# The last step's down products: the third PSUM bank from a pair of the up products

## The chip, the cores and the metric

The kernel runs on one core of a Trainium2 chip. The time is the device time of the whole program in microseconds (us); the medians are over several executions, and the profile is of one execution. PSUM is the memory that the matmuls write to; the kernel uses it as eight banks. The engines are TensorE (PE in the views; PEld is its load of a matmul's first operand, the weight load), VectorE (DVE), ScalarE (ACT), GpSimd (POOL) and SyncE (SP).

## The reference, cut to what matters

```python
# per batch and head: a linear attention with an RMS norm; x is its output, 4608 x 512
kv  = np.einsum('bhsd,bhse->bhde', k, v)
out = np.einsum('bhsd,bhde->bhse', q, kv)
x   = out / rms * g_norm                      # reshaped to (4608, 512)
# four experts, summed with the tokens' probabilities
for e in range(E):
    h = np.maximum(x @ w1[e], 0.0)            # "up",   512 -> 1024
    out += p[:, e:e + 1] * (h @ w2[e])        # "down", 1024 -> 512
```

All is float32. The change touches only the down product of the very last step.

## The kernel before

The work is 36 steps: 4 experts by 9 chunks of 512 tokens. (The prediction calls the last one step 35, its index from 0.) Each matrix product is made of seven smaller ones, numbered 1 to 7, from sums and differences of blocks. So the relu'd blocks h1, h2, ... need further adds: h3 = h2 - h6, for instance. Some of the products are split by seven once more (the "inner" products). A *merge* scales a finished product by the tokens' probabilities and adds it into the output rows, which frees its bank. A *pass* is one matmul record of the profile: each float32 matmul of the kernel shows as two.

A small list-scheduler in the kernel lays all operations out in order of time. A buffer belongs to a kind, and each kind has some slots. An operation can be placed only when a slot of the kind it needs is free, and an add marked `either` goes to VectorE or GpSimd, whichever the plan reaches first. So moving one buffer to another kind can reorder operations that the change does not name.

```python
BANKS = {"u1": 2, "u2": 2, "db": 2, "ab": 2}      # eight PSUM banks in four pairs
...
bank = {1: Buf("u1", ...), 2: Buf("u2", ...), 5: Buf("u2", ...)}        # up()
...
def either(n):
    return {"DVE": 0.155 + 0.00104 * n, "POOL": 0.15 + 0.00225 * n}
...
elif m == 4:                                                            # up(), the last part
    add(key, unit(2), made[1], made[4])             # h2; adds default to `either`
    relu(key, h[2])
    add(key, unit(3), h[2], h[6], ALU.subtract)     # h3
...
def down(s, e, c):            # each expert's last chunk, and all chunks of expert 0
    for t in range(2):        # two halves of the tokens
        for j, m in enumerate((1, 6, 5, 7, 4, 3, 2)):
            kind = "ab" if e and t else "db"
            if m == 1:
                banks[1] = Buf(kind, f"d1_{s}_{t}")      # holds products 1, 6, 7, 4
            elif m in (2, 5):
                banks[2] = Buf(kind, f"d{m}_{s}_{t}")    # 5 and then 3; for 2 a new one
            ps = banks[1 if m in (1, 6, 7, 4) else 2]
            ...  # four matmuls into ps[:, 0:256]; then a merge on VectorE into the output rows
```

The step just ahead of the last one uses the inner products. Its final group also lives in `db`: there the inner products 7 and then 4 share one bank, and between them ScalarE must copy 7 out (a "snapshot"). Other inner products hold the other bank.

Of the kernel before, what the change touches and what calls it, by code (L numbers as in the profile page):

```python
# [230 lines left out]
def kernel(  # L231
# [39 lines left out]
    E, DM, F = moe_w1.shape  # L271
# [5 lines left out]
    NCH = B + 1  # L277
# [58 lines left out]
    def pe(products, columns, passes=2):  # L336
        return {"PE": passes * products * (0.008 + 0.0008125 * columns) + 0.003}
# [506 lines left out]
    def four(b):  # L844

        return b.ap[:].rearrange("p (a b u t) -> p a b u t", a=2, b=2, u=2)
# [230 lines left out]
    def down(s, e, c):  # L1077
        h = hidden.pop(s)
        base = s + 1.2
        merge, send = result(s, e, c, base)  # L1080
        second = []
        for t in range(2):
            banks = {}
            for j, m in enumerate(MERGED):
                key = base + (7 * t + j + 0.5) / 14
                kind = "ab" if e and t else "db"
                if m == 1:
                    banks[1] = Buf(kind, f"d1_{s}_{t}")
                elif m in (2, 5):
                    banks[2] = Buf(kind, f"d{m}_{s}_{t}")  # L1090
                ps = banks[1 if m in (1, 6, 7, 4) else 2]

                def product(eng, m=m, t=t, ps=ps):
                    for kt in range(4):
                        nc.tensor.matmul(  # L1095
                            ps.ap[:, 0:HN], lhsT=four(h[m])[:, kt // 2, t, kt % 2, :],
                            rhs=w2f[e][m].ap[:, kt * HN:(kt + 1) * HN],
                            start=(m in (1, 2, 5) and kt == 0), stop=(kt == 3),
                            skip_group_check=True,
                        )  # L1100

                op = plan.add(
                    key, pe(4, HN), product, reads=[h[m], w2f[e][m]], writes=[ps],
                    after=second[-1:] if t and m in (1, 5) else (),
                )
                op.marks = ps, HN
                if m == 2:
                    second.append(op)
                i, half, fresh = {
                    1: (t, 0, True), 2: (t, 0, False), 6: (t, 1, True), 3: (t, 1, False),  # L1110
                    5: (2 + t, 1, True), 7: (2 + t, 1, False), 4: (2 + t, 0, True),
                }[m]
                merge(key - 0.4, [ps], lambda ps=ps: ps.ap[:, 0:HN], i, half, fresh)
            send(base + 0.5 * (t + 1), t)
            send(base + 0.5 * (t + 1), 2 + t)
# [171 lines left out]
    for e in range(E):  # L1287
        for c in range(NCH):
            s = e * NCH + c
# [14 lines left out]
            if e and c < NCH - 1:  # L1304
                if not primed:
                    banks = [Buf("ab", f"prime{i}") for i in range(2)]

                    def prime(eng, banks=banks):
                        for b in banks:
                            nc.tensor.matmul(b.ap[:, 0:P], lhsT=ident[:], rhs=ident[:], start=True,  # L1310
                                             stop=False, skip_group_check=True)
                            nc.tensor.matmul(b.ap[:, P:HN], lhsT=ident[:], rhs=ident[:], start=False,
                                             stop=True, skip_group_check=True)

                    primed.append(plan.add(s + 1.1, pe(4, P), prime, writes=banks))
                    primed[0].marks = banks[0], HN
                down_deep(s, e, c)
            else:
                down(s, e, c)
# [54 lines left out]
```

## Time and profile before

| | |
|---|---|
| time, median of 3 runs | 1731.64 us (1731.56 to 1731.66) |
| profiled span | 1729.4 us |
| TensorE busy | 1719.6 us, 99% |
| TensorE's share of the chain that ended last | 99% |
| from product 7's block (1698.08) to the start of the last merge (1724.86) | 26.78 us |
| from there to the end of the span (the trace has it as 1729.43) | 4.6 us |

The stretch that the change can touch starts at four passes of the previous step's product 7, line L1170, and ends with the last merge (line L1049). I call it the *tail*; starts are printed to 0.01 us, so a tail can be off by 0.01. Timelines give the start of an instruction or a merged run of them, its length in us, the engine, the line, what it writes and reads, and in brackets how long the engine was idle before it and who ended that.

### The profile page before, as it was taken

To read this page: it belongs to the slowest core of one execution; us is meant where nothing else is said; L and a number is where in the kernel's file an instruction comes from. 1 tells how busy PE (TensorE), PEld (TensorE's weight loads), DVE (VectorE), ACT (ScalarE), POOL (GpSimd) and SP (SyncE) were. 2 spreads that over 40 slices of the span, in tenths; PEclk is the share of its full clock that TensorE was granted. 3 is DMA by queue.
4 is the path that set the end of the run, shared out by engine and by line. 5 is a ranking of instruction groups with operands and counts; after the bars stand their busy time and mean duration, and the time that the engine had idled before them with its cause. 6 is when DMAs were issued, how large, how long until landed. Compare 5 with 4: busy or idle time off the path is not lost.

```text
span 1729.4 us, 38448 instructions
## 1 busy us (share of the span) xinstructions
PE 1719.6 (99%) x15334; PEld 1652.0 (96%) x15334; DVE 1222.8 (71%) x1968; ACT 938.6 (54%) x2300; POOL 616.5 (36%) x561
## 2 busy tenths in 40 slices
PE   9999999999999999999999999999999999999998
PEld 7699999999999999999999999999999999999997
DVE  4755655565676777777788877777788877777774
ACT  3354544454444565656555556566555556665652
POOL 3421323133334333333345333333345333333331
PEclk9999999999999999999999999999999999999999
DMA  9756444633333343534465344444475344444442
GB/s 240 218 161 193 153 122 131 193 135 128 147 130 99 94 114 104 116 106 113 131 185 110 99 110 111 111 111 110 114 204 110 98 111 111 110 110 109 112 99 49
DMA packets 148596, 220.94 MB, mean 128 GB/s; under 512 B 49600, under 2 KB 90816, under 8 KB 148416
## 3 DMA queue, kind: packets, MB, share of 16 engines
q1 hardware_dynamic: 133312, 191.21, 35.6%
q0 software_dynamic: 15104, 27.27, 11.0%
q8 instruction: 120, 1.97, 0.5%
q14 instruction: 60, 0.49, 0.1%
HBM read 145.30 MB, written 73.14 MB: 126 GB/s over the span
## 4 chain that ended last, share of the span: by engine, by line
PE 99%; POOL 0%; ACT 0%; DVE 0%; issue 0%; POOLq 0%
PE u L881 45%; PE db L1170 19%; PE db L1095 15%; PE ab L1170 12%; PE ab L1095 2%; PE u L968 2%; PE ab L634 1%; PE ab L678 1%; PE ab L620 1%; PE ab L1323 1%; PE ab L660 1%; PE db L660 0%; POOL rt L551 0%; PE ab L722 0%; PE ab L704 0%; PE ab L738 0%
## 5 line engine op out<-in xcount | busy, mean ns | idle before, releaser
L360 DVE TENSOR_TENSOR big<-big,big 128x1024 f32<-128x1024 f32 (+1 forms) x449 | 440.9, 995 | 34.9 <-ACT big L864 23.8
L881 PE MATMUL u<-xf,big 128*128 128x128 f32 x3104 | 453.3, 276 | 0.0
L881 PEld LDWEIGHTS u<-xf,big 128*128 128x128 f32 x3104 | 401.5, 192 | 2.2
L881 PE MATMUL u<-xf,w1y 128*128 128x128 f32 x2652 | 389.9, 276 | 0.0
L908 DVE TENSOR_TENSOR big<-u,snap 128x256 f32<-128x256 f32 x430 | 181.3, 422 | 235.9 <-PE u L881 176.4
L881 PEld LDWEIGHTS u<-xf,w1y 128*128 128x128 f32 x2652 | 343.6, 192 | 2.1
L900 ACT ACTIVATE snap<-u 128x256 f32<-128x256 f32 x490 | 187.7, 383 | 251.6 <-PE u L881 212.2
L1095 PE MATMUL db<-big,big 128*128 128x256 f32 x1136 | 269.0, 382 | 2.1 <-DVE big L560 2.1
L1095 PEld LDWEIGHTS db<-big,big 128*128 128x128 f32 x1136 | 207.1, 192 | 25.4 <-DVE big L560 2.3
L900 ACT ACTIVATE big<-u 128x256 f32<-128x256 f32 x430 | 164.7, 383 | 110.6 <-PE u L881 75.5
L360 POOL TENSOR_TENSOR big<-big,big 128x256 f32<-128x256 f32 (+1 forms) x139 | 172.5, 1248 | 132.3 <-DVE big L360 46.8
L1170 PE MATMUL db<-big,big 128*128 128x128 f32 x1056 | 146.9, 276 | 0.4 <-ACT snap L1198 0.4
L864 ACT ACTIVATE big<-big 128x1024 f32<-128x1024 f32 x128 | 134.5, 1051 | 3.4 <-POOL big L360 2.1
L1170 PEld LDWEIGHTS db<-big,big 128*128 128x128 f32 x1056 | 132.1, 192 | 0.6 <-ACT snap L1198 0.6
L1236 POOL TENSOR_TENSOR big<-big 128x512 f32<-128x512 f32 x26 | 33.0, 1268 | 269.2 <-DVE big L360 263.9
L1198 ACT ACTIVATE snap<-db 128x256 f32<-128x256 f32 x192 | 68.4, 356 | 100.0 <-PE db L1170 95.1
L360 POOL TENSOR_TENSOR big<-big 128x512 f32<-128x512 f32 (+1 forms) x57 | 70.3, 1232 | 126.8 <-DVE big L360 102.6
L1170 PE MATMUL db<-kv,big 128*128 128x128 f32 x804 | 114.7, 275 | 0.0
L1065 POOL DMA_DIRECT2D out_dram<-big x100 | 91.2, 987 | 47.4 <-ACT snap L1198 22.8
L900 ACT ACTIVATE u<-u 128x256 f32<-128x256 f32 x245 | 90.9, 371 | 28.1 <-PE u L881 8.0
L1170 PEld LDWEIGHTS db<-kv,big 128*128 128x128 f32 x804 | 102.1, 192 | 0.1
L1206 DVE TENSOR_TENSOR big<-ab,snap 128x256 f32<-128x256 f32 x140 | 59.1, 422 | 57.4 <-ACT snap L1198 31.9
(213 smaller groups left out, 2676.9 us busy)
## 6 DMA issues: line engine op xcount, KB each, us to landing
xf<-x SPq DMA_DIRECT2D x108, 512.0 KB, 3.6
out_dram<-big POOLq DMA_DIRECT2D x84, 256.0 KB, 5.8
xf<-x_h SPq DMA_DIRECT2D x81, 256.0 KB, 3.2
xf<-x SPq DMA_DIRECT2D x81, 256.0 KB, 3.3
x<-xf SPq DMA_DIRECT2D x36, 512.0 KB, 6.1
big<-in_moe_w_dram SPq DMA_DIRECT2D x25, 512.0 KB, 4.8
small<-in_q_dram SPq DMA_DIRECT2D x72, 128.0 KB, 4.8
kv<-in_k_dram SPq DMA_DIRECT2D x30, 288.0 KB, 4.8
```

What stands on the lines that cost most here:

```text
L360: lambda eng: adder(eng).tensor_tensor(out=out_(), in0=a(), in1=b(), op=op),
L864: lambda eng: nc.scalar.activation(out=b.ap[:], in_=b.ap[:], func=ACT.Relu),
L881: nc.tensor.matmul(ps.ap[:, u * P:(u + 1) * P], lhsT=w1f[e][m][mm][1]()[:, u * P:(u + 1) * P], rhs=views[m][mm][1](), start=(mm in (1, 5) ...
L900: lambda eng: nc.scalar.activation(out=where(), in_=ps.ap[:, 0:HN], func=ACT.Copy),
L908: lambda eng: nc.vector.tensor_tensor(out=block(whole, a, t), in0=src.ap[:, 0:HN], in1=add_.ap[:], op=ALU.add),
L968: nc.tensor.matmul(bank.ap[:], lhsT=two(w.ap[:])[:, kt, ut * P:(ut + 1) * P], rhs=two(xh[dh].ap[:])[:, kt, :], start=(dh == kt == 0), stop ...
L1065: nc.gpsimd.dma_start(out=dst, in_=cell(i)[parts, :], accum_op=ALU.add)
L1095: nc.tensor.matmul(ps.ap[:, 0:HN], lhsT=four(h[m])[:, kt // 2, t, kt % 2, :], rhs=w2f[e][m].ap[:, kt * HN:(kt + 1) * HN], start=(m in (1, ...
L1170: nc.tensor.matmul(ps.ap[:, o * P:(o + 1) * P], lhsT=b.ap[:, col:col + P], rhs=w2q[e][m][mm][1]()[:, kt, :], start=(mm in (1, 5) and o == ...
L1198: lambda eng: nc.scalar.activation(out=where(), in_=group_of(ps.ap), func=ACT.Copy),
L1206: lambda eng: nc.vector.tensor_tensor(out=cell(tq, dq), in0=group_of(src.ap), in1=group_of(add_.ap), op=ALU.add,),
L1236: lambda eng: adder(eng).tensor_tensor(out=whole(to), in0=whole(a), in1=whole(b), op=ALU.add),
```

## The change

Its intent: the last step's products 5, 3 and 2 should not compete for the two `db` banks with the previous step's inner products. No up product follows, so the pair `u2` is idle.

```diff
                 elif m in (2, 5):
-                    banks[2] = Buf(kind, f"d{m}_{s}_{t}")
+                    banks[2] = Buf("u2" if s == E * NCH - 1 else kind, f"d{m}_{s}_{t}")
```

## The prediction

> **What bounds the kernel now.** I read the page's busy times and chain first, to see which engine sets the end; then the chain cut to the last 30 us, because the change touches only step 35 of 36; then the timeline of each engine there, for the size of every hole.
>
> ```profile
> PE 1719.6 (99%) x15334; PEld 1652.0 (96%) x15334; DVE 1222.8 (71%) x1968; ACT 938.6 (54%) x2300; POOL 616.5 (36%) x561
> PE 99%; POOL 0%; ACT 0%; DVE 0%; issue 0%; POOLq 0%
> ```
>
> TensorE works for 1719.6 of 1729.4 us and carries 99% of the chain. A change that removes no matmul can win at most the holes in its stream, 9.8 us over the whole span, and start and end of the program hold most of those. The chain at the end (start, duration, what):
>
> ```profile
> 1698.24 0.46 PE db L1170 x4
> 1698.70 0.02 issue
> 1698.72 0.28 ACT snap L1198
> 1699.01 0.04 issue
> 1699.05 1.16 PE db L1170 x8
> 1700.21 12.53 PE db L1095 x56
> 1712.74 12.10 PE ab L1095 x56
> 1724.84 0.02 issue
> 1724.86 0.48 DVE big L1049
> ```
>
> L1170 is the previous step's inner product, L1095 the last step's 14 down products of eight matmul passes. Equal numbers of passes took 12.53 and 12.10 us: a hole hides in the first seven. The TensorE timeline (start, us, what, idle before) and the weight loads size the holes:
>
> ```profile
> 1697.18 0.61 PE L1170 MATMUL db<-kv,big 128*128 128x128 f32 x4
> ...
> 1698.08 0.61 PE L1170 MATMUL db<-kv,big 128*128 128x128 f32 x4
> 1699.05 0.71 PE L1170 MATMUL db<-big,big 128*128 128x128 f32 x4 [0.36 <-ACT snap L1198]
> 1699.60 0.61 PE L1170 MATMUL db<-kv,small 128*128 128x128 f32 x4
> 1700.13 9.15 PE L1095 MATMUL db<-big,big 128*128 128x256 f32 x40
> ...
> 1712.57 8.80 PE L1095 MATMUL ab<-big,big 128*128 128x256 f32 x40
> ...
> 1705.56 3.32 PEld L1095 LDWEIGHTS db<-big,big 128*128 128x128 f32 x16 [0.39 <-DVE big L360]
> ```
>
> The undisturbed step from one block of four narrow passes to the next is 0.45 us (1697.18 to 1698.08 holds two such steps). So:
> - **Hole A**: the block at 1699.05 was due at 1698.53, 0.52 late. It then costs 0.55 to the next block instead of 0.45 (its first weight load is no longer hidden), 0.10 more. Together 0.62.
> - **Hole B**: the first down product was due at 1699.60 + 0.45 = 1700.05 and came at 1700.13, 0.08 late, plus about the same 0.10 for its exposed weight load: 0.18.
> - **Hole C**: 40 wide passes took 9.15 instead of 8.80, 0.35 more. 0.10 of it is B's weight load, so C is 0.25, at the weight load of 1705.56 that waited for a VectorE add.
>
> A + B + C = 1.05 us is all that exists in this stretch. The cause of C is one line of work:
>
> ```profile
> 1700.60 2.36 POOL L360 TENSOR_TENSOR big<-big,big 128x1024 f32<-128x1024 f32 x1 [0.69 <-ACT big L1042]
> 1702.99 1.06 ACT L864 ACTIVATE big<-big 128x1024 f32<-128x1024 f32 x1 [1.32 <-POOL big L360]
> 1704.29 1.22 DVE L360 TENSOR_TENSOR big<-big,big 128x1024 f32<-128x1024 f32 x1
> ```
>
> GpSimd forms h2, ScalarE applies the relu, VectorE forms h3 = h2 - h6, and product 3 waits for h3 until 1705.51 + 0.05.
>
> **What the skill says.** (1) PSUM — Partial Sum Buffer, section Terms: two engines must not be on one bank and quadrant at once, so a reused bank has to wait for its reader. The trace agrees in the ordering: A is product 4 of the previous step waiting until the snapshot of the same bank (0.28 us) is out, and B is the first down product waiting for that bank's next evacuation. (2) TensorE: Matmul & The Clock Gate, section The mechanism: matmuls are strictly in order, only weight loads are pulled ahead. The trace agrees: during A nothing else of TensorE's stream runs although product 5 of the last step had all its operands. What fills a hole must therefore stand in the hole in program order. (3) SBUF — State Buffer, section "SBUF: two separate sides": GpSimd and a VectorE operation with two SBUF inputs exclude each other on a shared port pair. A VectorE add of 128x512 (L1236) took 1.21 us beside a GpSimd add (1699.24, while GpSimd ran 1698.64 to 1699.91) and another of the same form 0.68 us alone (1702.97), so I ask below who is beside whom.
>
> **The change, part by part.** The list-scheduler lays the program out anew. Comparing both builds, all instructions up to the last step are the same and in the same order; the last 14 down products and a handful of neighbours move. No product, transfer or byte is added or removed.
>
> 1. *Product 5, first half, moves into hole A.* It now writes a bank of the second up pair, which no one uses, so it needs no wait and is placed between the previous step's products 7 and 4. Its 8 passes at 0.2157 (8.80 less the 0.38 tail of the last pass, over 39) last 1.73 us. Product 7 ends its issue at about 1698.52; product 4 then comes at about 1700.25, when the snapshot (out at 1699.00) is long done. A vanishes: -0.62.
> 2. *Hole B stays.* Products 4, 3 of the previous step and 1 of the last still use the same bank: issue of 4 ends 1700.69, 3 ends 1701.14, the copy of 4 starts about 0.31 after its last pass, at 1700.89, and releases product 1 at 1701.22, the same 0.08 late. ScalarE now has two L1042 copies ahead of it (1699.97 and 1700.37 as before, each about 0.40 start to start), free at about 1700.8, just in time. 0.
> 3. *The add for h2 moves from GpSimd (2.36 us) to VectorE (1.22 us),* right behind the L1236 add there, so from 1700.38 to 1701.60 instead of 1700.60 to 1702.95. No GpSimd add is beside it. The relu could start at 1701.65, but ScalarE first has the copy of product 4 (1700.89) and two L1042 copies (from about 1701.06 and 1701.46). It starts near 1701.87 and ends near 1702.93, 1.1 us earlier than before.
> 4. *Product 2 now comes second, and needs h2.* Product 1 starts 1701.22 and its eighth pass is issued at 1701.22 + 0.32 + 6 x 0.2157 = 1702.83. The weight load of product 2 may come at 1702.83 and is hidden up to about 0.11 later (C shows this: the load came 0.36 after the pass before it at 1705.20, but C is 0.25). Release at 1702.93 + 0.05 = 1702.98, so 0.15 late, less 0.11: a new hole D of 0.04. Uncertain by 0.15 either way, but it cannot go below 0.
> 5. *h3.* VectorE: relu out at 1702.93, h3 from 1702.98 to 1704.20, product 3 wanted at 1702.83 + 1.73 = 1704.56. Slack 0.3: C vanishes, -0.25.
> 6. *The rest of the products.* Each bank is reused with at least one other product (1.73 us) between; a merge on VectorE takes 0.48 and starts about 0.2 after the product's last pass, so no waits, as in the steady second half of before.
> 7. *After the last product* nothing changes: one merge, two stores of one row block, 5.0 us to the end of the span, with the previous two stores one product earlier, as now. 0.
>
> Sum: -0.62 - 0.25 + 0.04 = -0.83. From 1731.64 this gives 1730.8 us, 0.05%.
>
> **Rivals.**
> - *The hole moves.* ScalarE is the weak point: if its queue runs 0.4 us later than reckoned, or the h2 add is held behind another VectorE instruction by a full 0.5 us, D grows to 0.4 or 0.5 and half of the gain is spent: 1731.2. For it: product 2 has no slack at all, and four short copies lie before the relu. Against: the copies' operands are all there by 1700.5.
> - *All three holes close.* If the copy for product 1 came a little earlier, B and D would be 0: 1730.6. Against: it takes the same bank through the same three products, so 0.08 late is what its latency makes of it.
> - *VectorE blocks on the early merge.* The merge of product 5 now stands ahead of h3 and needs the reloaded output rows. If they were late, h3 and product 3 would be late and the change would lose. Against: these loads landed by 1674.7, 27 us earlier.
> - *The end is a store, not TensorE.* The stores already follow the last merge, so an earlier merge moves them along one for one; the GpSimd stores now start about 1.9 us sooner, having no 2.36 us add in front.
>
> **Range and chances.** Three runs of before lie within 0.10 us, so the size is readable, barely above that noise. All holes closed is 1730.6, the larger D is 1731.2; I widen both by 0.2 to 0.3 for another chip's offset, to 1730.3 and 1731.4. A 2% step would be 35 us, and the whole stretch that is changed is only 31 us long: both outer chances are almost nil.
>
> **What would show it.** Right: the step from product 7 to 4 has no idle time, the first L1095 line stands near 1698.5, the weight load waiting for L360 is gone, the VectorE h2 add takes about 1.22, the last merge starts near 1724.0. Wrong: a wait of product 2 for L864 of more than 0.3 us, a wait of product 3 for L360, a longer B, or a last merge that still starts near 1724.9.

## The result, and the profile after

| | before | after |
|---|---|---|
| first comparison, median us | 1731.60 (4 runs, 1731.13 to 1731.66) | 1730.51 (4 runs, 1729.95 to 1730.74) |
| second comparison, median us | 1731.34 (9 runs, 1730.91 to 1731.89) | 1730.52 (5 runs, 1730.35 to 1730.83) |
| tail in the profile, us | 26.78 | 25.92 |

The ratios of the fast runs are 0.9994 (95% interval 0.9977 to 1.0011) and 0.9996 (0.9983 to 1.0008): the same within 2%, as forecast. A ratio here is the mean time of one kernel's fast runs over that of the other's of the same rounds, so it is not quite the ratio of the medians. Neither interval excludes 1. No run of the changed kernel was as slow as the fastest of the kernel before in the same rounds (1730.74 against 1731.13, 1730.83 against 1730.91), but how much of that is the change only the traces show. All outputs are right.

TensorE's timeline of the changed kernel from product 7 on:

```profile
1697.70 0.61 PE L1170 MATMUL db<-kv,big 128*128 128x128 f32 x4
1698.15 1.89 PE L1095 MATMUL u<-big,big 128*128 128x256 f32 x8
1699.88 0.61 PE L1170 MATMUL db<-big,big 128*128 128x128 f32 x4
1700.32 0.61 PE L1170 MATMUL db<-kv,small 128*128 128x128 f32 x4
1700.85 1.99 PE L1095 MATMUL db<-big,big 128*128 128x256 f32 x8
1702.68 1.90 PE L1095 MATMUL u<-small,big 128*128 128x256 f32 x8
1704.42 1.89 PE L1095 MATMUL u<-big,big 128*128 128x256 f32 x8
```

Product 5 (the `u` line at 1698.15) stands between product 7 and product 4 of the previous step. It starts 0.45 us after the block of product 7, the undisturbed step, so hole A is gone. Product 1 at 1700.85 comes 0.53 after the block before it and is 0.10 longer than its fellows: hole B, as before. Product 2 at 1702.68 is 0.01 longer than the rest, which is all there is of hole D. Product 3 at 1704.42 comes 1.74 after it, so it waits for nothing.

The h2 add, the h3 add and the last merge of the changed kernel, from VectorE's timeline, and the relu between the adds, from ScalarE's:

```profile
1700.00 1.21 DVE L360 TENSOR_TENSOR big<-big,big 128x1024 f32<-128x1024 f32 x1
...
1702.57 1.22 DVE L360 TENSOR_TENSOR big<-big,big 128x1024 f32<-128x1024 f32 x1
...
1723.62 0.48 DVE L1049 SCALAR_TENSOR_TENSOR big<-u,p_all,big 128x256 f32<-128x256 f32 x1 [1.24 <-PE u L1095]
```

```profile
1701.50 1.04 ACT L864 ACTIVATE big<-big 128x1024 f32<-128x1024 f32 x1
```

The GpSimd add of 2.36 us is now a VectorE add of 1.21 us. This profile reached product 7 0.37 us sooner than the profile of before (1697.70 against 1698.08), ahead of anything that the change reorders; where this comes from is told in the section on why the prediction was right. With 0.37 added, all these times can be laid on the prediction's: 1700.37 for h2 (predicted 1700.38), 1701.87 for the relu (1701.87), 1702.94 for h3 (1702.98), 1723.99 for the last merge (1724.0).

### The profile page after: what moved, and what is told of

It reads as the page before. It is cut to its first block, busy times and chain, and to the rows that moved or that the text cites. A ratio compares the mean times of both kernels' runs of the same rounds, so it can differ in the third digit from the quotient of the medians.

```text
span 1728.2 us, 38444 instructions
## 1 busy us (share of the span) xinstructions
PE 1718.7 (99%) x15334; PEld 1651.4 (96%) x15334; DVE 1224.7 (71%) x1969; ACT 939.3 (54%) x2300; POOL 614.8 (36%) x560
## 4 chain that ended last, share of the span: by engine, by line
PE 99%; POOL 1%; DVE 0%; ACT 0%; issue 0%; POOLq 0%
PE u L881 45%; PE db L1170 19%; PE db L1095 14%; PE ab L1170 12%; PE ab L1095 2%; PE u L968 2%; PE ab L634 1%; PE ab L1323 1%; PE ab L620 1%; PE ab L678 1%; PE ab L660 1%; PE u L1095 1%; POOL rt L551 0%; PE db L660 0%; PE ab L722 0%; PE ab L704 0%
## 5 line engine op out<-in xcount | busy, mean ns | idle before, releaser
L1095 PE MATMUL db<-big,big 128*128 128x256 f32 x1120 | 264.1, 380 | 2.1 <-DVE big L560 2.1
L1095 PEld LDWEIGHTS db<-big,big 128*128 128x128 f32 x1120 | 202.9, 190 | 24.6 <-DVE big L560 2.3
L1170 PEld LDWEIGHTS db<-big,big 128*128 128x128 f32 x1056 | 132.1, 192 | 0.1
```

The lines of the kernel that those rows point to most:

```text
L1095: nc.tensor.matmul(ps.ap[:, 0:HN], lhsT=four(h[m])[:, kt // 2, t, kt % 2, :], rhs=w2f[e][m].ap[:, kt * HN:(kt + 1) * HN], start=(m in (1, ...
L1170: nc.tensor.matmul(ps.ap[:, o * P:(o + 1) * P], lhsT=b.ap[:, col:col + P], rhs=w2q[e][m][mm][1]()[:, kt, :], start=(mm in (1, 5) and o == ...
```

## The experiments

The theory: TensorE's stream sets the length of this stretch; the tail shrinks by exactly the holes that get filled (A 0.62, B 0.18, C 0.25), and a hole is filled by what stands in it in program order with its operands and bank ready. The rivals: the gain comes from the VectorE add alone; it needs the up pair's banks as such; part of the first difference of 1.09 us comes from elsewhere; B is no wait but the price of the turn from narrow to wide passes.

**1. The changed kernel again.** No edit.

> The changed kernel once more, beside the kernel before. Theory (hole A filled by product 5, hole C closed by the earlier h2): from the start of the previous step's product 7 (its block of four passes on the bank db) to the last merge it takes 25.9 us, against 26.8 of before, in every profile, and the difference of the medians comes to 0.9 us. Rival (part of the first difference of 1.09 us is the change acting elsewhere, earlier in the program): the difference of medians is again 1.1 us or more and the part before the last step is again 0.4 us shorter. If that part was only run to run scatter, it can come out with any sign.

The tail was 25.91 us (1698.61 to 1724.52), the medians 1730.52 and 1731.34, a difference of 0.82. Product 7 was reached at 1698.61, this time *later* than in the profile of before. So the rival falls: the extra 0.37 us of the first profile differs from run to run and is not the change.

**2. The first bank from an up pair too.** On top of the change:

```diff
-                    banks[1] = Buf(kind, f"d1_{s}_{t}")
+                    banks[1] = Buf("u1" if s == E * NCH - 1 else kind, f"d1_{s}_{t}")
```

> The changed kernel, and the last step's first bank is taken from the first up pair as well. Product 1 then fills hole A and the product after the previous step waits for no copy. Theory (holes cost their wait plus the exposed weight load): A, B and C all closed, D not there: product 7 to last merge 25.7 us, 0.2 less than the changed kernel, difference to before 1.07 us. Rival (hole B is a fixed cost of the turn from narrow to wide passes, no wait): 25.9 us, the same as the changed kernel.

```profile
1698.84 0.61 PE L1170 MATMUL db<-kv,big 128*128 128x128 f32 x4
1699.28 1.89 PE L1095 MATMUL u<-big,big 128*128 128x256 f32 x8
1701.01 0.61 PE L1170 MATMUL db<-big,big 128*128 128x128 f32 x4
1701.45 0.61 PE L1170 MATMUL db<-kv,small 128*128 128x128 f32 x4
1701.90 3.62 PE L1095 MATMUL u<-big,big 128*128 128x256 f32 x16
```

In this timeline of TensorE every step is 0.45 us, the one to 1701.90 included, and no group is longer than its passes. The last merge starts at 1724.55: a tail of 25.71 us, 0.2 less than the change. The turn from narrow to wide passes costs nothing here, so hole B was a wait plus an exposed weight load. Median 1730.14 (5 runs, 1729.50 to 1731.09), before 1731.34.

**3. Only the first bank.** The same line on the kernel *before*; the third bank stays in `db`.

> The kernel before, and only the last step's first bank is taken from the first up pair; the third bank and GpSimd's h2 add stay. Theory: product 1 fills hole A; products 6, 5 and 7 follow before the first one that needs h2, so the slow GpSimd add (2.4 us) is covered: all holes closed, 25.7 us. Rival (the gain needs the third bank, or the h2 add on VectorE): at most A is gone and C stays, 26.1 us or more.

The tail was again 25.72 us (1698.49 to 1724.21), with no hole. GpSimd still forms h2, from this kernel's timeline of GpSimd:

```profile
1701.01 2.35 POOL L360 TENSOR_TENSOR big<-big,big 128x1024 f32<-128x1024 f32 x1 [0.69 <-DVE big L1236]
```

So neither the third bank nor the faster h2 add is needed. Product 1 fills hole A; then products 6, 5 and 7 run, 1.73 us each, before product 2, the first that wants h2. Median 1729.57 (5 runs, 1729.53 to 1730.53), before 1731.34: a difference of 1.77, more than the tail's 1.06. The rest is not the edit's doing: four of the five runs had a granted TensorE clock of 1.000, none of the nine of before did, and the same kernel's median in experiment 10 is 1730.32.

**4. The third bank from `ab`.** On the kernel before:

```diff
-                    banks[2] = Buf(kind, f"d{m}_{s}_{t}")
+                    banks[2] = Buf("ab" if s == E * NCH - 1 else kind, f"d{m}_{s}_{t}")
```

> The kernel before, and the last step's third bank comes from the pair ab of the down products, idle too by then, in place of the up pair. Theory (any bank that is free when hole A opens will do): the same order of products as in the changed kernel and 25.9 us from product 7 to the last merge. Rival (the banks of the up pair matter as such, or ab is still held by the previous step's product 2): product 5 waits in hole A and some or all of 0.6 us comes back, 26.2 to 26.8 us.

Tail 25.91 us (1697.73 to 1723.64), the same holes as the change. So the pair does not matter, as long as it is free by then.

**5. Only the h2 add on VectorE.** On the kernel before; TensorE's order stays as it was.

```diff
-                add(key, unit(2), made[1], made[4])
+                add(key, unit(2), made[1], made[4], where=dve if s == E * NCH - 1 else either)
```

> The kernel before, and only the last step's h2 add is bound to VectorE; TensorE's order stays as it was. Theory: h3 is ready near 1704.2 in the time of before, 1 us ahead of product 3, so C closes and A and B stay: product 7 to last merge 26.5 us, 0.25 less than before. Rival (the earlier h2 is the whole of the gain): 25.9 us. Rival (C was a wait for something else): 26.8 us.

```profile
1698.25 0.61 PE L1170 MATMUL db<-kv,big 128*128 128x128 f32 x4
1699.23 0.71 PE L1170 MATMUL db<-big,big 128*128 128x128 f32 x4 [0.37 <-ACT snap L1198]
1699.78 0.61 PE L1170 MATMUL db<-kv,small 128*128 128x128 f32 x4
1700.31 8.90 PE L1095 MATMUL db<-big,big 128*128 128x256 f32 x40
```

Hole A is there with its 0.98 us step and its wait for the snapshot. The 40 wide passes take 8.90 us, where the kernel before took 9.15: exactly C's 0.25 is gone, and the 0.10 over 8.80 is B's weight load. Tail 26.54 us (1698.25 to 1724.79). The earlier h2 is worth C and nothing more.

**6. The changed kernel with the h2 add on GpSimd.** The same edit on the changed kernel, with `gp` in place of `dve`. The scheduler then puts product 6 behind product 1, on the same bank.

> The changed kernel, and the last step's h2 add is bound to GpSimd. Product 5 still fills hole A, but product 2 has no h2 and product 6 comes right after product 1 on the same bank. Theory: product 6 waits for product 1's merge, a new hole of 0.84 us (merge start 0.42 after the last pass, 0.48 long, 0.05 to release, less 0.11 hidden), up to 1.0 if VectorE's add of 128x512 is held by the GpSimd add; it eats A and C: 26.75 to 26.9 us, no better than before. Rival (filling A is a gain of its own, whatever comes after): 26.2 us or less.

From this kernel's timeline of TensorE, and then those of GpSimd and of VectorE:

```profile
1698.25 0.61 PE L1170 MATMUL db<-kv,big 128*128 128x128 f32 x4
1698.70 1.89 PE L1095 MATMUL u<-big,big 128*128 128x256 f32 x8
...
1704.13 1.99 PE L1095 MATMUL db<-big,big 128*128 128x256 f32 x8 [0.73 <-DVE big L1049]
```

```profile
1700.77 2.36 POOL L360 TENSOR_TENSOR big<-big,big 128x1024 f32<-128x1024 f32 x1 [0.69 <-DVE big L1236]
```

```profile
1701.91 1.76 DVE L1236 TENSOR_TENSOR big<-big,big 128x512 f32<-128x512 f32 x1
1703.60 0.47 DVE L1049 SCALAR_TENSOR_TENSOR big<-db,p_all,big 128x256 f32<-128x256 f32 x1
```

Hole A is filled here as in the change (1698.70 follows 1698.25 by 0.45), and yet the tail is 26.90 us (1698.25 to 1725.15), longer than before. Product 6 came 2.73 us after product 1 at 1701.40, in place of 1.83 (1.73 and the 0.10 of hole B), and its own weight load cost 0.10 more: a new hole of 1.00, the upper of the two values expected. Its length is explained by the VectorE lines: an add of 128x512 that takes 0.68 us alone took 1.76, ending 0.54 after the GpSimd add ended at 1703.13, and the merge that frees the bank had to queue behind it. Filling a hole is no gain of its own if the order that fills it makes another.

**7 and 8. The two halves of the change.** On the kernel before, the third bank from `u2` only for product 5, and only for product 2:

```diff
-                    banks[2] = Buf(kind, f"d{m}_{s}_{t}")
+                    banks[2] = Buf("u2" if s == E * NCH - 1 and m == 5 else kind, f"d{m}_{s}_{t}")   # 7
+                    banks[2] = Buf("u2" if s == E * NCH - 1 and m == 2 else kind, f"d{m}_{s}_{t}")   # 8
```

> Half of the change: only product 5 takes the bank of the up pair, product 2 keeps the bank of the down pair. Theory (it is product 5's place in hole A and the free bank then left for product 2 that count, not which bank product 2 has): 25.9 us, as the whole change. Rival (both halves are needed): 26.1 to 26.5 us.

> The other half: only product 2 takes the bank of the up pair, product 5 keeps the bank of the down pair. Nothing can go into hole A; product 2 goes ahead of 7 and 3, so product 3 comes 3.5 us later and h3 is in time although GpSimd forms h2. Theory: A and B stay, C closes: 26.5 us. Rival (A is closed by any third bank): 25.9 us.

Product 5 alone gives a tail of 25.91 us (1698.24 to 1724.15), the whole of the change. Product 2 alone gives 26.53 us (1698.09 to 1724.62): A and B are there, and only C is closed, because product 3 now comes two products later and h3 is in time.

**9 and 10. Past the last merge.** The third experiment's kernel, with the second store of each pair of the last step on ScalarE's queue, and that kernel again beside it on another chip.

```diff
-                for parts, dst in where:
+                for n, (parts, dst) in enumerate(where):
                     if e and not again:
                         nc.gpsimd.dma_start(out=dst, in_=cell(i)[parts, :], accum_op=ALU.add)
                     else:
-                        nc.sync.dma_start(out=dst, in_=cell(i)[parts, :])
+                        queue = nc.scalar if again and n else nc.sync
+                        queue.dma_start(out=dst, in_=cell(i)[parts, :])
```

> The third experiment's kernel (only the first bank moved), and of each pair of stores of the last step the second is issued by ScalarE's queue in place of SyncE's. With no hole left between the previous step and the end, the path behind the last merge is what remains: the two store issues there stand 0.51 us apart on one queue, and the program ends after the second has landed. Theory: from the last merge to the end of the span 4.0 us in place of 4.5, and 25.7 us before it as in the third experiment; 0.5 us less in the medians than the repeat of it. Rival (the two stores share something else, or the closing of the program has a fixed length): 4.5 us as before.

> The third experiment's kernel again on this chip, as the thing to compare the ninth with. Theory: 25.7 us from product 7 to the last merge, 4.5 us after it, about 1.1 us under the kernel before in the median, with single runs scattered by some 0.5 us as before.

Both have a tail of 25.72 us. From the last merge to the end of the span the ninth took 4.32 us (1724.08 to 1728.40) and the tenth 4.57 (1723.97 to 1728.54): 0.25 less, half of what was expected. The stores were issued together, but the one on ScalarE's queue landed later; the views of the DMA issues in the last 8 us (KB each, median us from issue to landing), the tenth and then the ninth:

```profile
out_dram<-big SPq DMA_DIRECT2D x4, 128.0 KB, 2.3
```

```profile
out_dram<-big SPq DMA_DIRECT2D x2, 128.0 KB, 2.3
out_dram<-big ACTq DMA_DIRECT2D x2, 128.0 KB, 2.6
```

The 0.5 us of issue is saved, and part of it is paid back in landing. The Trainium skill, DMA: Bandwidth & Descriptors, section "Issuing engines are not separate DMA queues", says that transfers of all issuing engines end up on the same 16 DMA engines and interleave; a second queue saves issue time only. The saved issue time fits these lines; no run here shows what made the landing slower. Medians: 1730.11 (5 runs, 1730.03 to 1730.20) for the ninth, 1730.32 (1729.69 to 1730.47) for the tenth, 1731.34 for the kernel before in the same rounds (9 runs, 1730.55 to 1733.48). The ninth's median is 0.21 us lower, which agrees with the 0.25 of the trace. One run of the tenth, 1729.69, lies below all of the ninth; it is the only one of the ten with a granted clock of 1.000.

All tails together:

| kernel | tail us | holes left |
|---|---|---|
| before | 26.78 | A, B, C |
| after | 25.92 | B |
| 1. after, again | 25.91 | B |
| 2. first and third bank moved | 25.71 | none |
| 3., 9. and 10. first bank moved | 25.72 | none |
| 4. third bank from `ab` | 25.91 | B |
| 5. h2 add on VectorE | 26.54 | A, B |
| 6. after, h2 add on GpSimd | 26.90 | B, and a new one of 1.00 |
| 7. only product 5 | 25.91 | B |
| 8. only product 2 | 26.53 | A, B |

## Why the prediction was right

The measured medians, 1730.51 and 1730.52, lie in the range of 1730.3 to 1731.4. They lie below 1730.6, though, the value for all holes closed, in the margin that was added for scatter: the steps were right, but that the number fell inside owes something to that margin. Step by step:

1. *Product 5 fills hole A, -0.62.* Right: in the changed kernel the step is 0.45 us. Product 5's new bank alone closes A (experiment 7), and the other parts of the change without it (experiments 5 and 8) leave it open. One remark in the prediction shows less than it says: in the kernel before, product 5 had its operands during A but no free bank, as the previous step held both of `db`; so that nothing ran in A is no test of the order.
2. *Hole B stays.* Right, 0.53 to product 1 in place of 0.45, and 0.10 more for its weight load. Experiment 2 shows that it is the wait for the bank, since it goes when the bank is changed. The prediction names the previous step's product 3 among those on this bank; by the kernel it is on the other one, and B is the wait for the copy of product 4 alone. The sum does not change.
3. *The h2 add moves to VectorE and takes 1.22.* Right: 1.21.
4. *A new hole D of 0.04.* It came out at 0.01. This is the only term of the sum that was off, by 0.03, inside its stated doubt of 0.15. The relu ended some 0.02 us earlier than reckoned.
5. *h3 in time, C vanishes, -0.25.* Right; experiment 5 isolates the 0.25.
6. *No further waits, 7. nothing new after the last merge.* Right: all later products stand 1.73 us apart, and the end took 4.6 us from the last merge in both (the 5.0 of the prediction is counted from the start of the last pass). GpSimd's stores started 2.15 us sooner, not 1.9; nothing of TensorE waited for them.

The sum was -0.83; the tail gave 26.78 - 25.92 = 0.86. The median lies 0.3 below the point forecast. The forecast started from 1731.64, the median of three runs of before; the medians of nine runs in the two later comparisons were 1731.34, and from there the sum gives 1730.51, which is what was measured. So the base was 0.3 high, and the terms were not.

The tail hardly depends on the run (25.71 or 25.72 in four profiles of three builds on two chips); what comes before it does. Product 7 was reached between 1697.70 and 1698.84 us in the twelve profiles, and up to there TensorE runs the same matmuls in the same order in all of them. The two earliest, 1697.70 (after) and 1697.73 (experiment 4), are the two with a granted clock of 1.000. In the other ten the trace has a stretch of 3.41 us, between 72 and 78 us from the start, in which half the clock was granted; from 74 to 76 us it was 0.50 in the kernel before and 1.00 in the changed one. The same product there, before and then after:

```profile
72.49 3.44 PE L1095 MATMUL db<-big,big 128*128 128x256 f32 x8 [2.10 <-DVE big L560]
```

```profile
73.81 1.99 PE L1095 MATMUL db<-big,big 128*128 128x256 f32 x8 [2.10 <-DVE big L560]
```

The profile of before was 1.32 us ahead until then and 0.37 behind from 78 us on, up to the last step: it lost 1.69 us there, and the 0.37 between the two profiles is what is left. What set off the stretch, and where the earlier lead came from, was not looked into.

The run times agree. Of the runs of before whose clock is on record, two had 1.000 and took 1730.55 and 1730.67; the other seventeen took 1730.91 or more. Among runs with a clock below 1.000 alone, the medians are 1731.34 for the kernel before (17 runs), 1730.52 for the changed one (8), 1730.39 for the first bank alone (5) and 1730.11 with two store queues too (5). Those differences to before, 0.82, 0.95 and 1.23 us, stand beside 0.86, 1.06 and 1.31 from the traces. They are pooled over rounds and chips, so they support the traces and do not replace them.

Of the rivals, "the hole moves" did not happen here (D was 0.01); experiment 6 made a new hole in another way, through a shared bank, and took the whole gain with it. "All three holes close" happens with another bank. "VectorE blocks on the early merge" did not happen: the merge of product 5 ran at 1701.43 with no wait of VectorE before it, and h3 followed the relu by 0.03 us. "The end is a store" is true of the last 4.6 us, and a change there is worth a further 0.25.

A version that beats both kernels came out: the first bank alone, from `u1` (experiment 3), is one line like the change, and leaves no hole; with the two store queues (experiment 9) it gives 1730.11 against 1731.34, 1.2 us. Here too the interval of the ratio (0.998 to 1.0005) includes 1; that it is better rests on the traces, 1.31 us under the kernel before.

## What to carry to other kernels

When one engine is 99% busy, list the holes in its stream with their sizes before judging a change: the sum of them is the ceiling for the stretch, and here it was 1.05 us of 1731 (1.06 to 1.07 was reached). A free buffer is worth the hole that it lets an independent piece of work stand in, and which work gets it matters: giving one to product 1 in place of product 5 closed all three holes here, because the products that then followed had their banks and inputs ready. When a scheduler decides the order, compare the orders of both builds first. Here the freed buffer also moved an add from GpSimd to VectorE; with the add held on GpSimd (experiment 6), two users of one bank came side by side and all of the gain was lost.

## What the Trainium skill lacked or had wrong

- TensorE: Matmul & The Clock Gate, "Back-to-back issue gap", gives its spacings without naming float32. Here each float32 matmul shows as two passes, and a pass of 128 columns came every 0.112 us and one of 256 columns every 0.216.
- The same page does not say what a late weight load costs. Here a wait before a block of four or eight passes was followed by 0.10 us more (a block of 0.71 in place of 0.61, a product of 1.99 in place of 1.89). A load that came 0.36 us after the wide pass before it cost 0.25 us in all (hole C); one that came 0.12 us after it cost 0.01 (product 2 of the changed kernel).
- PSUM — Partial Sum Buffer, Terms, has the rule that two engines must not be on one bank and quadrant at once, but no price for keeping to it. Here product 4 could follow product 7 on the same bank only 0.97 us after its start, in place of 0.45, with a copy of 0.28 us between.
- SBUF — State Buffer, "SBUF: two separate sides", says that VectorE and GpSimd exclude each other, but not how much of the later operation remains when the earlier one ends. Here VectorE's add of 128x512 took 0.68 us alone and 1.21 and 1.76 us beside GpSimd adds, ending 0.54 us after the GpSimd add in both cases.
- No page was found that says how the landing of a 128 KB store changes with a second queue at work: 2.6 us on ScalarE's against 2.3 on SyncE's, two stores each.
